# Both kv sums of a step pair ahead of both numerators, and a PSUM copy of the counts in the picks

## The chip, the cores and the metric

The kernel runs on one core of a Trainium2 chip. The metric is the device time of one execution in microseconds (us). The engines are TensorE (PE; its weight loads are shown apart as PEld), VectorE (DVE), ScalarE (ACT), GpSimd (POOL) and SyncE (SP), which issues most of the DMAs.

## What is computed

Linear attention with random features, and then a mixture of experts on its output. Cut to what matters:

```
phi(x):  proj = x @ w_phi                    # 64 -> 128 features
         proj = proj - max|proj| over features
         [exp(proj), exp(-proj)]             # 256 features
q_p, k_p = phi(q), phi(k)                    # 8 batches, 8 heads, 576 tokens
kv  = sum over tokens of k_p (outer) v       # 256 x 64 for each head
z   = sum over tokens of k_p
num = q_p @ kv                               # the numerators
den = q_p @ z + 1e-6
x   = num / den, as 4608 rows of 512
row is computed if x @ w_skip > 0; expert e = argmax(x @ w_gate) of 8
y   = gate * (relu(x @ w1[e]) @ w2[e]);  out = x + y for computed rows, else x
```

## The kernel before

**Units and steps.** The attention stage works on units: one batch, four heads, either of k or of q. There are 16 units of each kind, and each has five steps `i`: step 0 is the tail of 64 tokens a head, steps 1 to 4 are the main part (two pairs of heads, two halves of 256 tokens). Two streams of steps run at once, that of k and, six steps behind, that of q. The time step `t` counts through them.

**Stages of a step.** Each step passes through stages with fixed lags (`run_stage(lag, f)` picks the step whose turn it is): transposes of the inputs on DVE (`st_t`, L324 and L322); the projection on PE into one PSUM tile "P" for both streams (`st_proj`, L347), its largest absolute value and the subtraction of it on DVE (L354, L357); exponentials on ACT (for k L372 and L373, and sums of them for z on POOL, L380 to L386; for q PE first transposes, L393, then L399 and L400); and last the stage of use, `f_use`.

**Stage of use.** For a k step, `st_use_k` adds to the kv sum in PSUM bank "K" (L415; the tail's part L422 after steps 2 and 4), and after step 4 ACT copies the finished sum out (L426). For a q step, `st_use_q` makes the numerators and denominators in a PSUM bank "O" (L513; the tail of two batches together, in odd batches only, L492). Then `norm` on DVE adds 1e-6 (L464), inverts (L468) and multiplies (L475, L476), which frees the bank. There are two banks "O"; the z sums (L433), the stage that turns kv into the operand `kva` (L446, L450, copied by ACT at L451 and L454), the ranking of routed rows (L613, L657) and the picks use them too.

**Pairs.** From `t` = 8 to 77 two time steps are emitted together as a pair, in the order of the list `PAIR`: a letter is a stage and the number is the step of the pair. Its stage of use is `('U', 0), ('U', 1)`, and each `U` runs the k step and then the q step. So PE has: kv sum of the first step, numerators of the first, kv sum of the second, numerators of the second. Since a unit has five steps and the streams are six apart, the pairs repeat in five kinds: with numerators of the steps q 0,1 (kv sums k 1,2), q 2,3 (k 3,4), q 4,0 (k 0,1), q 1,2 (k 2,3) and q 3,4 (k 4,0). Step 0 of k has no kv sum of its own, and step 0 of q has numerators only in odd batches.

**Who sets the order.** Within `tc.manual_schedule` (from `t` = 8 to before 79) PE and ACT keep the order of the text. DVE, POOL and SP are ordered by a planner at build time, which estimates when each instruction is ready. Each engine carries out its instructions in order.

**Picks.** When the routed rows of the first six batches are counted, two experts are picked for early work (`pick(0)` at `t` = 77, within the pair of `t` = 76, and `pick(1)` at `t` = 79). A pick sums the counts `Stot` over partitions with one matmul into a bank "O" (L689). DVE then reads the counts three times (L695 for the largest, L696, and at L703 for the part that is taken) between other small steps (L697 to L700), and works out places and gathers (L706 to L720). The bank comes free after L703.

After the attention the expert stage begins at some 340 us: it loads weights by the chunk, splits them on ACT, DVE and POOL, and does the matmuls.

Of the kernel before, what the change touches and what calls it, by code (L numbers as in the profile page):

```python
# [11 lines left out]
I32 = mybir.dt.int32  # L12
# [6 lines left out]
P = 128  # L19
# [5 lines left out]
def kernel(  # L25
# [12 lines left out]
    nc = tc.nc  # L38
    B, H, S, D = q.shape
    NF = w_phi.shape[1]  # L40
    E = w_gate.shape[1]
# [23 lines left out]
    const = ctx.enter_context(tc.tile_pool(name="const", bufs=1))  # L65
# [14 lines left out]
    def bank(tag):  # L80
        if not ps:
            return psa.tile([P, 512], F32, tag=tag, name="ps_" + tag, bufs=CFG["na"][tag])
        return ps[0].tile([P, 512], F32, tag=tag, name="ps_" + tag, bufs=NB[tag])
# [17 lines left out]
    ones_b = const.tile([P, P], BF16, name="ones_b")  # L101
# [11 lines left out]
    Stot = const.tile([P, E], BF16, name="Stot")  # L113
# [3 lines left out]
    eid0 = const.tile([1, 3], I32, name="eid0")  # L117
    idg0 = const.tile([P, 3, 2], I32, name="idg0")
    pad0 = const.tile([P, 3, 2], I32, name="pad0")
    const.tile([1, 64], I32, name="spare")  # L120
    mark = const.tile([1, 32], I32, name="mark")[:, 0:1]

    ft = const.tile([P, NSL, 4], I32, name="ft")
# [132 lines left out]
    with actx:  # L256
# [17 lines left out]
        for b in range(B):  # L274
            for kind in ("k", "q"):
                for hq in range(NQ):
                    u = Unit()
# [260 lines left out]
        def sm(tag, shape, dt=F32, bufs=2):  # L538
            return small.tile([P] + shape, dt, tag=tag, name=tag, bufs=bufs)
# [145 lines left out]
        def pick(j):  # L685


            cn = bank("O")[:, 0:E]
            nc.tensor.matmul(cn, ones_b, Stot, start=True, stop=True)  # L689
            mx = sm("mx", [5])[:, 0:1]  # L690
            d = sm("d", [5, E])[:, 0]
            key = sm("key", [5, E])[:, 0]
            km = sm("km", [5])[:, 0:1]
            pk = pks[:, j]
            nc.vector.tensor_reduce(out=mx, in_=cn, axis=AX.X, op=ALU.max)  # L695
            nc.vector.tensor_tensor(out=d, in0=cn, in1=mx.broadcast_to([P, E]), op=ALU.subtract)  # L696
            nc.vector.scalar_tensor_tensor(out=key, in0=d, scalar=0.0, in1=desc, op0=ALU.is_equal, op1=ALU.mult)  # L697
            nc.vector.tensor_reduce(out=km, in_=key, axis=AX.X, op=ALU.max)
            nc.vector.tensor_tensor(out=pk, in0=key, in1=km.broadcast_to([P, E]), op=ALU.is_equal)
            nc.vector.tensor_scalar(  # L700
                out=eid0[:, j:j + 1], in0=km[0:1], scalar1=-1.0, scalar2=float(E), op0=ALU.mult, op1=ALU.add)
            cs = sm("cs", [E])
            nc.vector.scalar_tensor_tensor(out=cs, in0=cn, scalar=float(SLOT), in1=pk, op0=ALU.min, op1=ALU.mult)  # L703
            r = slice(32 * j, 32 * j + 1)
            with nc.allow_low_precision(reason="integers up to 256 are exact"):
                nc.vector.tensor_tensor(out=Stot[r], in0=Stot[r], in1=cs[r], op=ALU.subtract)  # L706
            a4 = acc4.rearrange("p (e s) -> p e s", s=4)
            a2 = acc.rearrange("p (e s) -> p e s", s=2)
            po = pk.rearrange("p (e o) -> p e o", o=1).broadcast_to([P, E, 2])
            tp = sm("tp", [2, E], bufs=1)  # L710
            ea = sm("ea", [2], bufs=1)
            nc.vector.tensor_tensor(
                out=tp.rearrange("p s e -> p e s"), in0=(a2 if j else a4)[:, :, 0:2], in1=po, op=ALU.mult)
            nc.vector.tensor_reduce(out=ea, in_=tp, axis=AX.X, op=ALU.add)
            places(idg0[:, j], pad0[:, j], ea)
            early.append(gather_rows(idg0[:, j], SLOT, NTE * P))
            if j == 0:
                nc.vector.tensor_tensor(out=a2, in0=a4[:, :, 2:4], in1=a4[:, :, 0:2], op=ALU.subtract)
                nc.vector.tensor_tensor(out=a2, in0=a2, in1=po, op=ALU.mult)
                nc.vector.tensor_tensor(out=a2, in0=a2, in1=a4[:, :, 0:2], op=ALU.add)  # L720
# [8 lines left out]
        n = len(streams[0][0])  # L729
        LP, LE, LU, LZ, LA = CFG["lag"]  # L730
        OFF = CFG["off"]
        streams = [(x[0], x[1], 0 if j == 0 else OFF) for j, x in enumerate(streams)]
        for dh in range(2):
            nc.scalar.dma_start(
                out=wsrc[dh * 64:dh * 64 + 64],
                in_=w_phi)
# [3 lines left out]
        def run_stage(lag, f):  # L740
            for items, us, off in streams:
                s = now[0] - off - lag
                if 0 <= s < n:
                    f(*items[s])

        def f_use(u, i):
            (st_use_k if u.kind == "k" else st_use_q)(u, i)

        def f_exp(u, i):
            (st_exp_k if u.kind == "k" else st_exp_q)(u, i)  # L750
# [9 lines left out]
                    if i == 0 and s // 5 + 1 < len(us):  # L760
                        st_load(us[s // 5 + 1])

        PAIR = [('L', 0), ('T', 0), ('T', 1), ('q', 0), ('k', 0), ('P', 0), ('P', 1), ('Z', 0), ('L', 1), ('q', 1), ('A', 0), ('k', 1), ('U', 0), ('U', 1), ('D', 0), ('D', 1)]
        man = None
        for t in range(n + OFF + LA):
            if CFG["man"] and t == CFG["man"][0]:
                man = ExitStack()
                man.enter_context(tc.manual_schedule(engines={mybir.EngineType.PE, mybir.EngineType.Activation}))
            if CFG["man"] and t == CFG["man"][1]:
                man.close()  # L770
            first = 8 <= t < 78 and (t - 8) % 2 == 0
            if 8 <= t < 78 and not first:
                continue
            for c, dt in PAIR if first else [(c, 0) for c in "L" + CFG["order"] + "D"]:
                now[0] = t + dt
                if c == "L":
                    for w, f in [x for x in later if x[0] <= now[0]]:
                        later.remove((w, f))
                        f()
                elif c in "ZA":  # L780
                    lag, f = (LZ, st_z) if c == "Z" else (LA, st_aug)
                    for lg in (LZ, LA) if first else (lag,):
                        run_stage(lg, f)
                elif c == "U":
                    run_stage(LU, f_use)
                elif c in "Eqk":
                    run_stage(LE, lambda u, i: f_exp(u, i) if c in ("E", u.kind) else None)
                elif c == "P":
                    st_proj()
                elif c == "D":  # L790
                    run_stage(LU - 3, lambda u, i: st_loadv(u) if (i == 0 and u.kind == "k") else None)
                    run_stage(CFG["vtl"], lambda u, i: st_loadvt(u) if (i == 0 and u.kind == "k") else None)
                else:
                    f_t()
            if t == CFG["at"]:
                setup_aug()
            if t == 1:
                setup()
# [175 lines left out]
    start = {"E": 0, "D": 0, "C": NSD, "S": NS2}  # L974
# [134 lines left out]
    for grp in CFG["seq"]:  # L1109
# [7 lines left out]
        for which, w, n in how:  # L1117
            for _ in range(n):
                x = slots[which]
                c = done.get((x, w), 0)  # L1120
# [34 lines left out]
    T, ready, parted = [], [], []  # L1155
# [46 lines left out]
    with tc.manual_schedule():  # L1202
# [4 lines left out]
        for k, (w, x, c) in enumerate(steps):  # L1207
            kind, i = x
# [95 lines left out]
```

## Time and profile before

| What | Value |
|---|---|
| Time, median of 3 runs | 605.47 us (602.71 to 608.13) |
| The profiled execution: time, span | 607.32 us, 605.4 us |
| Mean granted TensorE clock | 0.975 |
| Attention stage | from 0 to some 340 us |

A row of a group or a wait names engine, line and tiles as out<-in; a wait has its sum in us, the number of times and the longest. A row of the timeline has its start and its length in us, then engine, line, operation and tiles, and xN where N instructions of the same kind are merged; in brackets stands the engine's idle time ahead of it and what ended it. The busy time of an engine is the union of its instructions; matmuls overlap, so the start of the next group tells more of a group's cost than its length.

### The profile page before, as it was taken

To read this page: it belongs to the slowest core of one execution; us is meant where nothing else is said; L and a number is where in the kernel's file an instruction comes from. 1 tells how busy PE (TensorE), PEld (TensorE's weight loads), DVE (VectorE), ACT (ScalarE), POOL (GpSimd) and SP (SyncE) were. 2 spreads that over 40 slices of the span, in tenths; PEclk is the share of its full clock that TensorE was granted. 3 is DMA by queue.
4 is the path that set the end of the run, shared out by engine and by line. 5 is a ranking of instruction groups with operands and counts; after the bars stand their busy time and mean duration, and the time that the engine had idled before them with its cause. 6 is when DMAs were issued, how large, how long until landed. Compare 5 with 4: busy or idle time off the path is not lost. (4 is left out here: it accounts for less than half of the span.)

```text
span 605.4 us, 18715 instructions
## 1 busy us (share of the span) xinstructions
PE 561.3 (93%) x7486; PEld 469.8 (78%) x7486; DVE 498.1 (82%) x1085; ACT 329.0 (54%) x649; POOL 375.4 (62%) x399
## 2 busy tenths in 40 slices
PE   4699999999999999999789799899999998999993
PEld 2477887777877788777667799798998987988892
DVE  5779998999989999899898749866789887867841
ACT  3266665665556555565453544345658665656720
POOL 5465567586675866848665635995567674638021
PEclk9799999999999999999899899899999999999997
DMA  9898898876778657521335297489787688777500
GB/s 158 155 156 166 190 196 181 189 135 138 164 160 189 124 142 180 121 74 46 106 106 184 71 300 268 155 289 310 202 284 227 232 288 297 244 224 261 193 20 30
DMA packets 250233, 108.33 MB, mean 179 GB/s; under 512 B 192417, under 2 KB 235553, under 8 KB 250144
## 3 DMA queue, kind: packets, MB, share of 16 engines
q1 hardware_dynamic: 245632, 97.58, 61.7%
q0 software_dynamic: 3200, 9.45, 4.3%
q8 instruction: 60, 0.98, 0.7%
q10 hardware_dynamic: 1312, 0.08, 0.1%
q14 instruction: 29, 0.24, 0.1%
HBM read 83.86 MB, written 24.02 MB: 178 GB/s over the span
## 5 line engine op out<-in xcount | busy, mean ns | idle before, releaser
L380 POOL TENSOR_TENSOR z<-ek 128x512 f32<-128x512 f32 x64 | 81.1, 1274 | 83.1 <-ACT ek L373 66.0
L200 POOL TENSOR_TENSOR w<-wraw_c,w 128x256 fp32r<-128x256 f32 x108 | 98.8, 947 | 49.6 <-ACT w L195 49.5
L195 ACT ACTIVATE w<-wraw_c 128x1024 fp32r<-128x1024 f32 x96 | 97.8, 1051 | 5.8 <-DMA wraw_c<-in_moe_w_dram 5.8
L200 DVE TENSOR_TENSOR w<-wraw_c,w 128x1024 fp32r<-128x1024 f32 x69 | 91.7, 1344 | 9.4 <-ACT w L195 8.2
L354 DVE TENSOR_REDUCE m<-ps_P 128x8 f32<-128x1024 f32 (+2 forms) x86 | 88.7, 1032 | 2.8 <-PE ps_P L347 2.8
L357 DVE TENSOR_TENSOR u<-ps_P,m 128x1024 f32<-128x1024 f32 (+2 forms) x86 | 88.5, 1029 | 2.3
L347 PE MATMUL ps_P<-wsrc,xT 64*64 64x128 f32 x2048 | 75.2, 283 | 14.2 <-DVE u L357 7.3
L513 PEld LDWEIGHTS ps_O<-kva,eq 128*64 128x64 f32 x2048 | 74.6, 138 | 16.3 <-DVE cs L703 4.7
L513 PE MATMUL ps_O<-kva,eq 128*64 128x74 f32 x2048 | 77.6, 230 | 6.7 <-DVE cs L703 4.1
L399 ACT ACTIVATE eq<-ps_U 128x512 f32<-128x512 f32 x64 | 38.2, 596 | 83.5 <-PE ps_U L393 82.5
L347 PEld LDWEIGHTS ps_P<-wsrc,xT 64*64 64x64 f32 x2048 | 59.5, 138 | 25.8 <-issue 14.7
L415 PE MATMUL ps_K<-ek,v 128*64 128x256 f32 x512 | 70.3, 394 | 0.0
L889 POOL DMA_INDIRECT out_dram<-o,si x22 | 32.4, 1474 | 57.1 <-DVE si L888 50.5
L956 PE MATMUL ps_O<-w,hh 128*128 128x512 f32 x160 | 64.2, 401 | 0.5 <-DVE o L903 0.5
L637 POOL TENSOR_SCALAR OP<-iota_p,rkp,wcol 128x128 bf16<-128x128 f32 x62 | 48.6, 795 | 13.4 <-DVE rec L468 7.2
L324 DVE STREAM_TRANSPOSE xT<-raw 128x512 f32<-128x512 f32 x64 | 43.9, 697 | 8.6 <-PE ps_P L347 4.5
L393 PE MATMUL ps_U<-ident,u 128*128 128x128 f32 x288 | 49.7, 291 | 0.3 <-DVE den L464 0.3
L372 ACT ACTIVATE ek<-u 128x512 f32<-128x512 f32 x64 | 41.0, 641 | 16.5 <-DVE u L357 9.7
L960 PE MATMUL ps_O<-w,hh 128*128 128x512 f32 x120 | 47.4, 395 | 0.1
L961 PE MATMUL ps_O<-w,hlo 128*128 128x512 f32 x120 | 47.3, 394 | 0.0
L415 PEld LDWEIGHTS ps_K<-ek,v 128*64 128x64 f32 x512 | 33.5, 139 | 16.5 <-issue 7.1
L386 POOL TENSOR_TENSOR z<-z,ekt 64x512 f32<-64x512 f32 x32 | 40.8, 1275 | 5.2 <-DMA xg<-xrows,idg 2.9
(254 smaller groups left out, 1203.6 us busy)
## 6 DMA issues: line engine op xcount, KB each, us to landing
wraw_c<-in_moe_w_dram SPq DMA_DIRECT2D x96, 512.0 KB, 5.3
raw<-in_k_dram SPq DMA_DIRECT2D x64, 144.0 KB, 3.2
raw<-in_q_dram SPq DMA_DIRECT2D x64, 144.0 KB, 3.6
v<-in_v_dram SPq DMA_DIRECT2D x64, 128.0 KB, 2.8
out_dram<-xm SPq DMA_DIRECT2D x16, 512.0 KB, 5.2
xrows<-xm SPq DMA_DIRECT2D x8, 516.0 KB, 3.9
xrows<-xm SPq DMA_DIRECT2D x8, 512.0 KB, 4.6
vt<-in_v_dram SPq DMA_DIRECT2D x32, 32.0 KB, 3.5
```

Of the source, the lines that this page charges most:

```text
L195: nc.scalar.activation(out=hi, in_=raw, func=AF.Copy)
L200: eng.tensor_tensor(out=lo[:, r], in0=raw[:, r], in1=hi[:, r].bitcast(F32), op=ALU.subtract)
L347: nc.tensor.matmul(p[s * 64:s * 64 + 64, hd, (nj + j) * NF:(nj + j + 1) * NF], xT[r, g * P + s * 64:g * P + s * 64 + 64], wsrc[r], start=T ...
L354: nc.vector.tensor_reduce(out=m.rearrange("p (j h) -> p j h", h=2), in_=pv, axis=AX.X, op=ALU.max, apply_absolute_value=True)
L357: nc.vector.tensor_tensor(out=uu[:, 0:2 * nj, :].rearrange("p (j h) f -> p j h f", h=2), in0=pv, in1=m.rearrange("p (j h o) -> p j h o", h ...
L380: zeng.tensor_tensor(out=z, in0=e[:, 0:2, :], in1=e[:, 2:4, :], op=ALU.add)
L393: nc.tensor.transpose(t[:, tt * P:(tt + 1) * P], uu[:, tt, :], ident)
L415: nc.tensor.matmul(o[hd * 64:hd * 64 + 64, :], u.v[:, 2 * hd + pr, g * D:(g + 1) * D], u.e[i][:, 2 * j + hd, :], start=(g == 0), stop=False,)
L513: nc.tensor.matmul(ov[s * 64:s * 64 + 64, 2 * j + hd, :], e[:, half, j, hd, s * 64:s * 64 + 64], kva[:, half, 2 * pr + hd, :], start=(half ...
L637: (nc.vector if last else nc.gpsimd).tensor_scalar(out=OP[:, t0 + t, c, :], in0=iota_p, scalar1=rkp[:, t:t + 1], scalar2=wcol[:, NT:NT + 1 ...
L956: nc.tensor.matmul(y[sub], hh[:, t], wh[:, fi, :], start=first, stop=False)
L960: nc.tensor.matmul(y[sub], hh[:, t], wl[:, fi, :], start=False, stop=False)
```

## The change

The stage of use is split. In a pair, `u` runs the k steps alone and `n` the q steps alone, so PE has now: kv sum of the first step, kv sum of the second, numerators of the first, numerators of the second. Outside the pairs the stage `U` is as it was. In `pick` the matmul's result is copied from PSUM to a new small tile in SBUF with one DVE copy, and the three reads go to that tile. The tile takes 2 x 32 bytes a partition, and an unused spare tile is made 64 bytes smaller.

```diff
-    const.tile([1, 64], I32, name="spare")
+    const.tile([1, 48], I32, name="spare")
...
-            cn = bank("O")[:, 0:E]
-            nc.tensor.matmul(cn, ones_b, Stot, start=True, stop=True)
+            cp = bank("O")[:, 0:E]
+            nc.tensor.matmul(cp, ones_b, Stot, start=True, stop=True)
+            cn = sm("cn", [E])
+            nc.vector.tensor_copy(out=cn, in_=cp)
...
-        PAIR = [('L', 0), ('T', 0), ('T', 1), ('q', 0), ('k', 0), ('P', 0), ('P', 1), ('Z', 0), ('L', 1), ('q', 1), ('A', 0), ('k', 1), ('U', 0), ('U', 1), ('D', 0), ('D', 1)]
+        PAIR = [('L', 0), ('T', 0), ('T', 1), ('q', 0), ('k', 0), ('P', 0), ('P', 1), ('Z', 0), ('L', 1), ('q', 1), ('A', 0), ('k', 1), ('u', 0), ('u', 1), ('n', 0), ('n', 1), ('D', 0), ('D', 1)]
...
-                elif c == "U":
-                    run_stage(LU, f_use)
+                elif c in "Uun":
+                    run_stage(LU, lambda u, i: f_use(u, i) if c == "U" or (c == "u") == (u.kind == "k") else None)
```

## The prediction

> **What bounds the kernel now.** I read the page first, then the busy time by stretches, the waits of TensorE (PE) and of VectorE (DVE), and last the timeline around single pairs and around the two picks.
>
> ```profile
> span 605.4 us, 18715 instructions
> PE 561.3 (93%) x7486; PEld 469.8 (78%) x7486; DVE 498.1 (82%) x1085; ACT 329.0 (54%) x649; POOL 375.4 (62%) x399
> 75.71:153.07 77.36, 74.74 (x1489) 60.36 (x1487) 73.32 (x182) 46.07 (x109) 54.71 (x51) 1.00 0.80 171
> ```
>
> The third row has a stretch, its length, the busy time of PE, its weight loads, DVE, ACT and POOL, then granted clock, DMA share and GB/s. It is one period of the attention stage: ten pairs, two batches, in 77.36 us (7.7 us a pair). PE is busy 74.74 of them and DVE 73.32, so both are nearly full: what is given back to one counts only where the other is not the later one. ACT and POOL have room. The change lies in these pairs, which run to about 297 us; the expert stage behind 340 us is not touched.
>
> ```profile
> PE ps_O L513 <- DVE cs L703: 4.1, 2, 3.1
> PE ps_O L513 <- ACT kva L454: 2.3, 7, 0.3
> PE ps_O L492 <- ACT kva L454: 0.9, 3, 0.3
> DVE den L464 <- PE ps_O L513: 2.5, 6, 0.4
> ```
>
> These are PE's waits from 20 to 330 us and, in the last row, DVE's from 40 to 285 us (sum, times, longest). Three of PE's rows are what the change can reach: numerators (L513, L492) that wait for the kva copies, 2.3 + 0.9 = 3.2 us, and for the picks' last read of their PSUM bank, 4.1 us.
>
> **The reordering: PE's own time.** I name a pair by the steps of its numerators (0 is the tail, L492). The kv sums are L415 and L422. This is pair q 1,2 at 95.9 us:
>
> ```profile
> 95.91 1.08 PE L415 MATMUL ps_K<-ek,v 128*64 128x256 f32 x8
> 96.82 0.60 PE L422 MATMUL ps_K<-ekt,vt 128*64 128x256 f32 x4
> 97.25 1.20 PE L513 MATMUL ps_O<-kva,eq 128*64 128x74 f32 x32
> 98.28 1.03 PE L415 MATMUL ps_K<-ek,v 128*64 128x256 f32 x8
> 99.14 1.20 PE L513 MATMUL ps_O<-kva,eq 128*64 128x74 f32 x32
> 100.27 0.66 PE L393 MATMUL ps_U<-ident,u 128*128 128x128 f32 x4
> 266.19 1.95 PE L415 MATMUL ps_K<-ek,v 128*64 128x256 f32 x16
> 267.97 0.60 PE L422 MATMUL ps_K<-ekt,vt 128*64 128x256 f32 x4
> 268.40 1.20 PE L513 MATMUL ps_O<-kva,eq 128*64 128x74 f32 x32
> 104.48 2.22 PE L513 MATMUL ps_O<-kva,eq 128*64 128x74 f32 x64
> 106.63 0.66 PE L393 MATMUL ps_U<-ident,u 128*128 128x128 f32 x4
> ```
>
> From first start to the start of what follows it takes 100.27 − 95.91 = 4.36 us. The other rows show the new sequence in places where the present kernel has it already (a step without tail work on one side): 16 sums before the sums' tail take 267.97 − 266.19 = 1.78, the tail 268.40 − 267.97 = 0.43, two numerators in a row 106.63 − 104.48 = 2.15; together 4.36 us. PE's own work costs the same in either order: 0.
>
> **The reordering: what becomes late.** The first numerator starts later by the second sum: 99.14 − 98.28 = 0.86 us, and 0.43 more where that sum has its tail (pairs q 2,3 and q 0,1). DVE's norm (L464, L468, L475, L476) follows it:
>
> ```profile
> 98.21 0.92 DVE L357 TENSOR_TENSOR u<-ps_P,m 128x768 f32<-128x768 f32 x1
> 99.05 0.15 DVE L464 TENSOR_SCALAR den<-ps_O 128x4 f32<-128x4 f32 x1
> 100.39 0.16 DVE L464 TENSOR_SCALAR den<-ps_O 128x4 f32<-128x4 f32 x1 [0.42 <-PE ps_O L513]
> 158.21 1.20 PE L513 MATMUL ps_O<-kva,eq 128*64 128x74 f32 x32
> 160.04 1.23 DVE L357 TENSOR_TENSOR u<-ps_P,m 128x1024 f32<-128x1024 f32 x1
> 161.28 0.15 DVE L464 TENSOR_SCALAR den<-ps_O 128x4 f32<-128x4 f32 x1
> 150.58 1.42 PE L492 MATMUL ps_O<-kva,eqt 128*64 128x74 f32 x31 [0.30 <-ACT kva L454]
> 154.52 0.15 DVE L464 TENSOR_SCALAR den<-ps_O 128x4 f32<-128x4 f32 x1
> 166.71 1.25 PE L513 MATMUL ps_O<-kva,eq 128*64 128x74 f32 x32 [0.33 <-ACT kva L454]
> 169.44 0.15 DVE L464 TENSOR_SCALAR den<-ps_O 128x4 f32<-128x4 f32 x1
> ```
>
> In pair q 2,3 (158.21) the numerator ends at 159.41 and the norm starts at 161.28, behind DVE's subtraction of the second projection (L357): 1.87 us of slack against 0.86 + 0.43 = 1.29. In q 0,1 the slack is 154.52 − 152.0 = 2.5 against 1.29, in q 4,0 169.44 − 167.96 = 1.48 against 0.86. Only q 1,2 is short: 99.05 − 98.45 = 0.60 against 0.86. The norm there would start about 0.3 later, and DVE loses nothing, because before the second norm it stands 0.42 us anyway until the second numerator ends, and that end does not move: the idle time goes from before the second norm to before the first. That takes DVE's order as it is; PE and ACT have theirs by hand, DVE's is laid by the planner, but the norms come behind both subtractions in the program's text too. Pair q 3,4 has no second sum and stays as it is.
>
> What becomes early: the second kv sum, by 98.28 − 97.25 = 1.03 us. Its input is two ACT exponentials from earlier in the pair, its v was loaded pairs ago, and no row of PE's waits names either. ACT's copy of a finished sum (L426) moves forward with it; ACT's next work is an exponential that waits for PE's next transposes, so nothing follows. This stage issues no DMA, and SP and POOL have nothing moved past them.
>
> **The kva waits.** In the rows at 150.58 and 166.71 the numerator comes straight behind the kva copies, or with one sum between. Now one or two sums (0.86 us or more) stand there first, so all ten waits, 3.2 us, should go. But the norms behind those numerators start 1.5 to 2.5 us after them: DVE is the later engine there, and PE only runs further ahead. Bounds: −3.2 us if PE set the pace, 0 if DVE does; I take 0, by the slack in these rows.
>
> **The picks.** Each pick holds one of the two "O" banks from its matmul to L703, and the second numerator of the pair wants that bank.
>
> ```profile
> 292.96 0.16 DVE L696 TENSOR_TENSOR d<-ps_O,mx 128x8 f32<-128x8 f32 x1
> 293.97 1.10 DVE L699 TENSOR_TENSOR pks<-key,km 128x8 f32<-128x8 f32 x1
> 295.33 2.24 PE L513 MATMUL ps_O<-kva,eq 128*64 128x74 f32 x32 [3.11 <-DVE cs L703]
> 297.62 0.16 DVE L464 TENSOR_SCALAR den<-ps_O 128x4 f32<-128x4 f32 x1 [1.24 <-PE ps_O L513]
> 299.12 0.71 DVE L324 STREAM_TRANSPOSE xT<-raw 128x512 f32<-128x512 f32 x1 [0.56 <-PE ps_P L347]
> 305.69 1.25 PE L513 MATMUL ps_O<-kva,eq 128*64 128x74 f32 x32 [0.94 <-DVE cs L703]
> 302.00:306.00 4.00, 3.06 (x62) 2.07 (x63) 3.93 (x13) 3.17 (x7) 3.84 (x4) 1.00 0.00 0
> 295.33:298.70 3.37, 3.37 (x48) 3.05 (x52) 1.93 (x15) 0.15 (x1) 2.16 (x2) 0.58 0.17 32
> 93.47 0.19 DVE L661 COPY acc<-ps_O 128x32 f32<-128x32 f32 x1 [0.46 <-PE ps_O L657]
> 303.03 1.18 DVE L697 SCALAR_TENSOR_TENSOR key<-d,desc 128x8 f32<-128x8 f32 x1
> 291.23 2.48 POOL L380 TENSOR_TENSOR z<-ek 128x512 f32<-128x512 f32 x2
> 293.79 1.26 POOL L384 TENSOR_TENSOR z<-z 128x512 f32<-128x512 f32 x1
> ```
>
> (i) Bank freed early. PE stands 3.11 us at the first pick, and the granted clock is 0.58 in the 3.37 us behind it, where 32 numerators take 2.24 us instead of 1.20. With the bank free after one copy both should go. What reaches the end is DVE's idle time that this causes: 1.24 us before the norm and 0.56 before the next transpose, together **−1.80**. At the second pick PE stands 0.94 us, but DVE is busy 3.93 of the 4.00 us around it, so nothing is late for DVE there: bounds −0.94 and 0, taken 0.
>
> (ii) The copies. Two PSUM copies; the trace has none of 8 columns, the nearest is L661's of 32 columns, 0.19 us. **+0.38**, all on DVE.
>
> (iii) The later reads. d (L696) and cs (L703) read the counts from SBUF now, so both of their inputs lie there. d from PSUM took 0.16; but small steps with both inputs in SBUF took 1.10 (L699) and 1.18 (L697), and they end where one of POOL's adds ends: L699 at 295.07, the add of 293.79 at 295.05. So four instructions may each wait for an add. Bounds: 0 (as from PSUM) to 4 × (1.18 − 0.16) = 4.1. By these rows: at the first pick d would wait from 292.96 to the adds' end at 293.71, the key for the add up to 295.05, and pks, which had waited for that anyway, would end some 0.4 later than now; at the second pick the key and L699 stand at POOL's adds already, so about 0.2 more. **+0.6**, an estimate from these rows.
> The Trainium skill (GPSIMD Engine Reference, Key points) says the same against this change: GpSimd shares its SBUF interfaces with VectorE and contends with DVE instructions that have two SBUF inputs. It also has a rule for the change (VectorE: DVE Perf Modes, Rules for kernel authors): copy PSUM to SBUF first where many operations follow. By that rule the four reads would get cheaper, by less than the 0.16 each that they take, and the sum would be about 1 us lower; the rows of L697 and L699 speak against it.
>
> The first spare tile shrinks by what the new small tile takes; no instruction touches it: 0.
>
> **The sum.** The profiled execution took 607.32 us, 1.9 more than its span, and is 1.85 above the median of 605.47. 0 (PE's order) + 0 (late norms) + 0 (kva waits) − 1.80 + 0.38 + 0.6 = −0.8: 606.5 for that execution, and against the median 604.7. From about 340 us on the expert stage waits for the last numerators, so I count what is gained before as kept.
>
> **Rivals.**
> *PE sets the pace.* Then all of PE's waits count: 3.2 + 4.1, and the slow clock behind the first pick (2.24 − 1.20 = 1.0): 8.3 us, 597.2. For it: PE's 74.74 us are more than DVE's 73.32 in the period. Against it: the norms' slack above, and DVE's waits for numerators sum to 2.5 us in 245 us.
> *POOL's adds hold the picks.* All four SBUF reads wait for a whole add (4.1) and the copies come on top (0.38), while the gain falls to 0, since DVE is then still in the pick when PE's numerators are done: 605.5 + 4.5 = 610.0. It decides once d and cs cost 1.80 − 0.38 = 1.4 us more than now. For it: L697 and L699. Against it: POOL's adds leave gaps (none follows the one at 293.79), and instructions that had waited for an add do not wait twice.
> *DVE's order is laid anew, to the worse.* The planner may see other ready times and lay the first norm ahead of the second subtraction. DVE would then stand until the first numerator ends: in q 1,2 from 98.21 to 98.45 + 0.86 = 99.31, 1.1 us; in q 2,3 from 160.04 to 159.41 + 1.29 = 160.70, 0.66 us. Six of each (the waits row counts six of 0.42 in q 1,2): 10.6 us, 615.3 with the −0.8. It decides from the first pairs on, if L464 stands before L357. Against it: in every pair of this kernel it stands behind, as in the text.
> *The copy does not free the bank early:* it lands where L695 stood or behind the subtraction after it, at 292 to 293 us; the second numerator would start near 292.5 in either case, so this is nearly the forecast.
>
> **How the numbers follow.** Forecast 604.7 with 0.60; PE sets the pace, 597.2, with 0.14; POOL's adds, 610.0, with 0.13; DVE's order, 615.3, with 0.10; something unseen, such as the planner's new order after 300 us, 0.03. The forecast's own range, by its bounds −1.8 − 0.94 + 0.38 and the other way with twice the reads' estimate, and by the spread of the runs shown (602.71 to 608.13), is 602 to 608. About 1% is what a measurement of this kernel can tell from no change: under 599.4 is faster, over 611.5 slower. Faster: 0.14 and a little of the forecast's edge, 0.15. Slower: DVE's order and a little of the unseen, 0.12. Same: 0.73. The range for 8 in 10 reaches towards the first two rivals: 599 to 610.
>
> **What would show it.** In the changed profile PE's waits for kva (L454) before numerators are gone, and PE's wait for the picks is under 0.5 us at the first, with the granted clock at full behind it. In q 1,2 DVE's idle time stands before the first norm (about 0.3) and hardly before the second. In the ten-pair period nothing changes beyond 0.3 us, though PE's waits shrink: DVE stays full. d and cs show whether they read at 0.16 or wait for POOL. I am wrong if the period shortens by 0.5 us or more (PE set the pace, or DVE's order got better), if L464 comes ahead of L357, or if the numerators' stage ends later than now.

## The result and the profile after

| | Time, median (lowest to highest) | Runs |
|---|---|---|
| before | 604.88 us (602.71 to 608.13) | 18 |
| after | 608.06 us (605.89 to 612.33) | 18 |

The ratio is 1.0054, with a 95% interval from 1.0041 to 1.0068. The changed kernel is slower by some 3.2 us. That is inside the range given and under 1%, but the forecast was a gain.

The profiled execution of the changed kernel took 605.89 us and is the fastest of its 18; that of before took 607.32. So the two spans must not be compared. Stretches inside them can be, because up to the last numerators the changed kernel repeated itself within 0.06 us in a second profile (see the experiments). From the profile page of after:

```profile
PE 557.8 (92%) x7486; PEld 467.0 (77%) x7486; DVE 502.0 (83%) x1087; ACT 328.5 (54%) x649; POOL 374.3 (62%) x399
```

PE is busy 3.5 us less than before and DVE 3.9 us more. As a ruler I take the starts of the large subtractions on DVE (L357; 86 in each kernel, counted from 0). From number 22 to 72 is the pairs' stretch, from 72 to 85 the tail's stretch, with both picks in it. Busy time by stretches, first of before, then of after (columns as in the prediction):

```profile
82.68:276.47 193.79, 187.06 (x3720) 150.78 (x3714) 183.61 (x452) 115.39 (x275) 137.18 (x125) 1.00 0.68 152
276.47:332.18 55.71, 49.79 (x850) 36.93 (x848) 50.54 (x149) 26.98 (x62) 38.32 (x38) 0.97 0.34 107
```

```profile
81.24:276.96 195.72, 185.81 (x3712) 150.45 (x3712) 185.93 (x452) 115.04 (x275) 135.75 (x124) 1.00 0.70 155
276.96:333.43 56.47, 51.77 (x851) 38.26 (x848) 52.44 (x151) 26.30 (x61) 38.27 (x38) 0.94 0.34 105
```

The pairs lose 195.72 − 193.79 = 1.93 us and the tail 0.76, together 2.69 of the 3.2 measured. In the pairs DVE does the same number of instructions (452) and is busy 2.32 us longer. Fifty subtractions are two and a half of the ten-pair periods, so a period is 0.8 us longer, where the prediction allowed 0.3 for no change. What PE waits for in after, from 20 to 330 us (sum, times, longest):

```profile
PE ps_O L657 <- DVE den L464: 5.2, 3, 1.8
...
PE ps_O L433 <- POOL z L386: 1.6, 1, 1.6
PE ps_O L433 <- DVE rec L468: 1.3, 1, 1.3
```

No row of this view names kva any more, and none a pick's step. PE waits for DVE in other places instead (the first row; in before 1.9 us), and new are the waits of the z sum (L433), which has no row in this view of before. Pair q 1,2 of after, in the timeline:

```profile
97.06 2.22 PE L513 MATMUL ps_O<-kva,eq 128*64 128x74 f32 x64
98.30 0.16 DVE L464 TENSOR_SCALAR den<-ps_O 128x4 f32<-128x4 f32 x1 [0.24 <-PE ps_O L513]
99.33 0.16 DVE L464 TENSOR_SCALAR den<-ps_O 128x4 f32<-128x4 f32 x1
```

All 64 numerators stand in one row. The idle time stands before the first norm (0.24 us) and hardly before the second (99.33 − 99.05 − 0.19 = 0.09), as forecast.

**Where the pairs lose.** In the pairs q 2,3, which also rank rows (L613 to L646). The pair of an odd batch, first before (its rows at 160.04 and 161.28 stand in the prediction), then after:

```profile
155.00 0.60 ACT L399 ACTIVATE eq<-ps_U 128x512 f32<-128x512 f32 x1 [3.08 <-PE ps_U L393]
...
159.87 0.14 DVE L624 TENSOR_TENSOR Stot<-Stot,st 128x8 bf16<-128x8 bf16 x1
159.91 1.27 POOL L386 TENSOR_TENSOR z<-z,ekt 64x512 f32<-64x512 f32 x1
...
161.19 0.18 DVE L633 TENSOR_REDUCE rki<-rm 128x4 int32<-128x32 f32 x1
...
161.47 0.17 DVE L634 TENSOR_SCALAR rkp<-rki 128x4 int32<-128x4 int32 x1
161.55 0.17 DVE L640 TENSOR_SCALAR RKH<-rki 128x4 int32<-128x4 int32 x1
161.62 0.17 DVE L468 RECIPROCAL rec<-den 128x4 f32<-128x4 f32 x1
161.75 0.64 DVE L646 SCALAR_TENSOR_TENSOR rm<-RKH,OH 128x32 bf16<-128x32 int32 x4
...
163.53 1.22 DVE L354 TENSOR_REDUCE m<-ps_P 128x8 f32<-128x1024 f32 x1
```

```profile
153.14 0.60 ACT L399 ACTIVATE eq<-ps_U 128x512 f32<-128x512 f32 x1 [2.33 <-PE ps_U L393]
...
158.06 1.26 POOL L386 TENSOR_TENSOR z<-z,ekt 64x512 f32<-64x512 f32 x1
158.75 0.60 DVE L624 TENSOR_TENSOR Stot<-Stot,st 128x8 bf16<-128x8 bf16 x1
...
160.50 0.17 DVE L633 TENSOR_REDUCE rki<-rm 128x4 int32<-128x32 f32 x1
160.77 0.17 DVE L634 TENSOR_SCALAR rkp<-rki 128x4 int32<-128x4 int32 x1
160.85 0.17 DVE L640 TENSOR_SCALAR RKH<-rki 128x4 int32<-128x4 int32 x1
161.05 0.63 DVE L646 SCALAR_TENSOR_TENSOR rm<-RKH,OH 128x32 bf16<-128x32 int32 x4
161.56 0.15 DVE L464 TENSOR_SCALAR den<-ps_O 128x4 f32<-128x4 f32 x1
...
163.24 1.21 DVE L354 TENSOR_REDUCE m<-ps_P 128x8 f32<-128x1024 f32 x1
```

Two things are seen. First, the planner laid the first norm's two small steps behind the ranking's. Before, den stood between rki and rkp, and rec between RKH and rm. A small step that needs the one just ahead starts 0.18 to 0.27 us after it (160.50 to 160.77), an independent one 0.07 to 0.1 (161.47 to 161.55); den and rec had filled such gaps. From L633 to the next L354 it took 163.53 − 161.19 = 2.34 us and takes 163.24 − 160.50 = 2.74: 0.40 more. In the pairs of even batches as much is lost, but it is won back in the next pair, where DVE had stood for PE before: from the subtraction at 127.36 us to that at 134.19 it took 6.83 us, in after 6.38 (126.70 to 133.08).

Second, in the pairs of odd batches the small add into Stot (L624) takes 0.60 us instead of 0.14; two such adds lie in the pairs' stretch. This one ends at 159.35, POOL's add of 158.06 at 159.32. Before, it fell just ahead of POOL's add of 159.91. POOL is earlier because PE is. In the pair ahead, from the first kv sum to the transposes (L393) behind the numerators, PE takes 4.36 us (148.09 to 152.45); before, with a wait for kva between, it took 5.12 (149.19 to 154.31). ACT's exponentials follow at 153.14 instead of 155.00, 1.86 us earlier, while DVE's L354 ahead of L624 is only 1.11 earlier (157.64 against 158.75).

**Where the tail loses.** The timeline around the picks, before and after (lines behind L690 count two more in after):

```profile
292.08 0.96 DVE L357 TENSOR_TENSOR u<-ps_P,m 128x768 f32<-128x768 f32 x1
...
301.04 1.22 DVE L357 TENSOR_TENSOR u<-ps_P,m 128x1024 f32<-128x1024 f32 x1
...
308.69 1.23 DVE L357 TENSOR_TENSOR u<-ps_P,m 128x1024 f32<-128x1024 f32 x1
...
312.74 0.18 DVE L572 TENSOR_TENSOR d<-L,mx 128x32 f32<-128x32 f32 x1
```

```profile
291.48 2.33 PE L513 MATMUL ps_O<-kva,eq 128*64 128x74 f32 x64
292.54 0.96 DVE L357 TENSOR_TENSOR u<-ps_P,m 128x768 f32<-128x768 f32 x1
293.60 0.62 DVE L698 TENSOR_TENSOR d<-cn,mx 128x8 f32<-128x8 f32 x1
299.87 1.22 DVE L357 TENSOR_TENSOR u<-ps_P,m 128x1024 f32<-128x1024 f32 x1
301.38 0.62 PE L433 MATMUL ps_O<-z,ones_f 128*32 128x256 f32 x4 [1.29 <-DVE rec L468]
302.34 1.26 POOL L386 TENSOR_TENSOR z<-z,ekt 64x512 f32<-64x512 f32 x1 [3.28 <-ACT ek L373]
303.65 1.07 PE L433 MATMUL ps_O<-z,ones_f 128*32 128x256 f32 x4 [1.65 <-POOL z L386]
307.63 1.23 DVE L357 TENSOR_TENSOR u<-ps_P,m 128x1024 f32<-128x1024 f32 x1
310.29 0.95 POOL L213 DMA_INDIRECT xg<-xrows,idg  x1 [0.30 <-issue]
310.65 1.93 DVE L572 TENSOR_TENSOR d<-L,mx 128x32 f32<-128x32 f32 x1
311.25 1.28 POOL L380 TENSOR_TENSOR z<-ek 128x512 f32<-128x512 f32 x1
302.60:309.40 6.80, 5.75 (x68) 4.46 (x72) 6.67 (x13) 2.08 (x6) 6.41 (x6) 0.50 0.00 0
```

The last row is one of the busy time by stretches. The first pick gives what it promised: its numerators run on without a wait, and from its subtraction to the next large one it takes 299.87 − 292.54 = 7.33 us instead of 301.04 − 292.08 = 8.96, a gain of 1.63. But from the subtraction at 307.63 to the stretch's end (333.43) it takes 25.80 us, before 332.18 − 308.69 = 23.49: 2.31 go there. PE, no longer late, now stands at the z sum, twice, and the granted clock is 0.50 in the 6.80 us from 302.60 on; DVE is busy 6.67 of these, so most of it is hidden. Openly on DVE's path stands L572 with 1.93 us instead of 0.18. The planner laid it ahead of the next largest value (L354, at 312.51); before, it stood behind that one (311.61). There it meets an add on POOL and ends 0.05 us after it (311.25 + 1.28 = 312.53). Between the two subtractions around it (307.63 to 313.84, before 308.69 to 312.93) 1.97 of the 2.31 us are lost.

### The profile page after: what moved, and what is told of

The parts are those of the page before. It is cut to its first block, busy times and chain, and to the rows that moved or that the text cites. A ratio compares the mean times of both kernels' runs of the same rounds, so it can differ in the third digit from the quotient of the medians.

```text
span 603.9 us, 18716 instructions
## 1 busy us (share of the span) xinstructions
PE 557.8 (92%) x7486; PEld 467.0 (77%) x7486; DVE 502.0 (83%) x1087; ACT 328.5 (54%) x649; POOL 374.3 (62%) x399
## 5 line engine op out<-in xcount | busy, mean ns | idle before, releaser
L354 DVE TENSOR_REDUCE m<-ps_P 128x8 f32<-128x1024 f32 (+2 forms) x86 | 88.6, 1031 | 2.8 <-PE ps_P L347 2.8
L357 DVE TENSOR_TENSOR u<-ps_P,m 128x1024 f32<-128x1024 f32 (+2 forms) x86 | 88.4, 1028 | 2.2
L513 PEld LDWEIGHTS ps_O<-kva,eq 128*64 128x64 f32 x2048 | 73.3, 138 | 10.4 <-DVE rm L631 3.1
L513 PE MATMUL ps_O<-kva,eq 128*64 128x74 f32 x2048 | 75.9, 229 | 2.8 <-DVE rm L631 2.0
L415 PE MATMUL ps_K<-ek,v 128*64 128x256 f32 x512 | 69.0, 396 | 0.0
L891 POOL DMA_INDIRECT out_dram<-o,si x22 | 31.1, 1415 | 55.8 <-DVE si L890 49.2
L393 PE MATMUL ps_U<-ident,u 128*128 128x128 f32 x288 | 49.4, 290 | 0.0
L386 POOL TENSOR_TENSOR z<-z,ekt 64x512 f32<-64x512 f32 x32 | 40.7, 1272 | 5.6 <-ACT ek L373 3.3
```

The costliest lines, as they stand in the source:

```text
L354: nc.vector.tensor_reduce(out=m.rearrange("p (j h) -> p j h", h=2), in_=pv, axis=AX.X, op=ALU.max, apply_absolute_value=True)
L357: nc.vector.tensor_tensor(out=uu[:, 0:2 * nj, :].rearrange("p (j h) f -> p j h f", h=2), in0=pv, in1=m.rearrange("p (j h o) -> p j h o", h ...
L393: nc.tensor.transpose(t[:, tt * P:(tt + 1) * P], uu[:, tt, :], ident)
L415: nc.tensor.matmul(o[hd * 64:hd * 64 + 64, :], u.v[:, 2 * hd + pr, g * D:(g + 1) * D], u.e[i][:, 2 * j + hd, :], start=(g == 0), stop=False,)
L513: nc.tensor.matmul(ov[s * 64:s * 64 + 64, 2 * j + hd, :], e[:, half, j, hd, s * 64:s * 64 + 64], kva[:, half, 2 * pr + hd, :], start=(half ...
```

## The experiments

Theory A was that the pairs lose by DVE's order in the rank pairs and by the add into Stot; B that the copies lay the tail's order anew; C that the loss lies in the expert stage. Stretches are from the one profiled execution of each, times and ratios from all runs, each ratio against the kernel before on the same chip.

| Kernel | Median, us | Ratio, 95% interval | Pairs' stretch | Tail's stretch |
|---|---|---|---|---|
| before | 604.8 to 605.3 | 1 | 193.79 | 55.71 |
| after | 608.06 | 1.0054 [1.0041, 1.0068] | 195.72 | 56.47 |
| after, once more | 608.48 | 1.0061 [1.0038, 1.0083] | 195.78 | 56.43 |
| reordering alone | 606.56 | 1.0022 [1.0005, 1.0039] | 195.86 | 56.04 |
| copies alone | 604.40 | 0.9998 [0.9980, 1.0016] | 193.71 | 55.27 |
| old order in rank pairs | 606.16 | 1.0021 [1.0004, 1.0039] | 194.51 | 57.58 |
| copy in first pick alone | 604.38 | 0.9986 [0.9970, 1.0003] | 193.80 | 54.72 |
| den in its gap | 605.95 | 1.0022 [1.0002, 1.0042] | 194.53 | 56.40 |
| den and counts in gaps | 605.87 | 1.0005 [0.9982, 1.0028] | 193.24 | 56.47 |
| den and counts in gaps, copy in first pick alone | 603.80 | 0.9989 [0.9973, 1.0006] | 193.21 | 55.93 |
| after, z add ahead of gathers | 611.38 | 1.0110 [1.0091, 1.0129] | 195.81 | 56.82 |
| den and counts in gaps, copy in first pick alone, z add | 602.94 | 0.9964 [0.9952, 0.9977] | 193.16 | 54.05 |
| copy in first pick alone, z add | 602.58 | 0.9960 [0.9945, 0.9975] | 193.74 | 53.60 |

Times do not follow the two stretches to the microsecond. With the reordering alone they are 2.40 us longer than before and the median 1.4; with the old order in the rank pairs 2.59 and 1.0; with the z add moved in the changed kernel 3.13 and 6.05. What the stage behind them adds in each kernel, no run here shows.

**The reordering alone.** The picks and the spare tile are those of before:

```diff
-            cp = bank("O")[:, 0:E]
-            nc.tensor.matmul(cp, ones_b, Stot, start=True, stop=True)
-            cn = sm("cn", [E])
-            nc.vector.tensor_copy(out=cn, in_=cp)
+            cn = bank("O")[:, 0:E]
+            nc.tensor.matmul(cn, ones_b, Stot, start=True, stop=True)
```

> The pairs have both kv sums first, the picks are as before the change. Theory A (the loss sits in the pairs that also rank a batch's rows: the planner lays the first norm behind the rank's small steps there, about 0.4 us each of six, and in every second one the add to Stot meets a POOL add, about 0.45 us): 2.4 to 3.3 us slower than before, 607.3 to 608.2, and in the trace the subtractions L357 fall back by some 0.85 us per ten pairs from 73 to 286 us. Theory B (the loss comes from the copies, which make the planner lay the work after 300 us anew): within 1 us of before, 604 to 606. Theory C (the loss is in the expert stage, by the phase in which it starts): no fall-back in the pairs.

The whole loss of the pairs is here (195.86), without any copy. The median's 1.4 us are less than the 2.4 to 3.3 that A gave.

**The copies alone.** The list of stages is that of before:

```diff
-        PAIR = [..., ('k', 1), ('u', 0), ('u', 1), ('n', 0), ('n', 1), ('D', 0), ('D', 1)]
+        PAIR = [..., ('k', 1), ('U', 0), ('U', 1), ('D', 0), ('D', 1)]
```

> The copies in both picks alone, the pairs as before the change. Theory A: 0 to 1.6 us faster than before, 603.3 to 605.0. Theory B: 1.5 to 2.7 us slower, 606.4 to 607.6. In both, PE's stand of 3.1 us at the first pick and the slow clock behind it go.

The pairs are as before (193.71); of the picks' gain 0.44 us is left at the end of the tail (55.27), too little for the runs to tell. The time is within A's range, and the 1.5 us or more that B put on the copies didn't come. What B said of the order did come: the order on POOL in the tail is that of the changed kernel and not that of before, and L572 stands ahead of L354 here too. In all thirteen traces the same holds: L572 stands ahead of L354 in the seven of kernels that copy in both picks, and behind it in the six others.

**The old order in the rank pairs.** The changed kernel, but pairs q 2,3 have the stage `U` of before:

```diff
+        PAIR_U = PAIR[:12] + [('U', 0), ('U', 1), ('D', 0), ('D', 1)]
...
-            for c, dt in PAIR if first else ...
+            for c, dt in (PAIR_U if (t - 10) % 5 == 2 else PAIR) if first else ...
```

> The changed kernel, but the pairs with numerators q 2,3 (all that rank a batch) keep sum, numerators, sum, numerators; DVE's order in them is then that of before. Theory A: the 2.5 to 3.3 us come back, 604.8 to 605.6. Theory B: as the changed kernel, 608. A half of it each way would say that only the waits for kva or the other pairs matter.

The pairs' stretch falls to 194.51: 1.21 of the 1.93 us come back. This changes PE's order and DVE's there together, so it does not say which. The add into Stot still takes 0.60 us in the odd batches (at 159.38 and 237.25), although its pair has the old order: PE runs ahead in the pairs between, and POOL with it. So the rest of the loss stays. The tail, whose text is the changed kernel's, came out 1.1 us longer, and the median is neither A's nor B's.

**The copy in the first pick alone**, and the rest as before:

```diff
+            cn = cp
+            if j == 0:
+                cn = sm("cn", [E])
+                nc.vector.tensor_copy(out=cn, in_=cp)
```

> The copy in the first pick alone, the second as before the change, the pairs as before. All that is laid behind the second pick stays as it was. Theory A and B: PE's 3.1 us and DVE's idle 1.8 us at the first pick go, less 0.6 for the copy and the reads: 1.0 to 1.8 us faster than before, 603.1 to 603.9. If POOL's adds hold the pick's reads: no gain or up to 1 us slower.

The tail's stretch is 54.72, 0.55 less than with both copies. That is 0.99 us less than before, and the median 0.8, a little less than forecast; the interval of the ratio just reaches 1.

**The changed kernel once more**, beside the next three.

> The changed kernel once more, beside the variants below. All theories: slower than before by 0.3 to 0.7%. In the profile the stretch from the 22nd to the 72nd of the large subtractions on DVE (some 50 to 292 us after the start of the span, to be called the pairs' stretch) is 195.7 us long again, against 193.8 before; if it is 194.0 or less, the loss in the pairs was chance and the order of DVE has nothing to do with it.

Both stretches come out within 0.06 us of the first time. So the loss in the pairs is no chance.

**DVE's order mended, PE's kept.** The rest of `rank` is traced behind den, with an edge on DVE that holds it there; the count goes with it. PE, ACT, POOL and SP keep the changed kernel's order to the instruction:

```diff
-            nc.vector.tensor_scalar(
-                out=den.rearrange("p (t o) -> p t o", o=1), in0=o[:, :, NA1:NAUG],
-                scalar1=1e-6, scalar2=None, op0=ALU.add,
-            )
+            den_i = nc.vector.tensor_scalar(out=den.rearrange("p (t o) -> p t o", o=1), in0=o[:, :, NA1:NAUG], scalar1=1e-6, scalar2=None, op0=ALU.add)
+            while pend:
+                with tc.issue_after(den_i.ins):
+                    list(pend.pop(0))
...
-                nc.vector.tensor_scalar(out=rkp[:, 0:nt], ...
+                yield; nc.vector.tensor_scalar(out=rkp[:, 0:nt], ...
...
-                for n, f in zip(CFG["post"], (rank, index, rest)):
+                for n, f in zip(CFG["post"], (lambda: (pend.append(rank()), next(pend[-1])), index, rest)):
```

> The changed kernel, with the two steps den (L464) ahead of rkp (L634) in the pairs that rank rows, and the count's two steps (L623, L624) among the steps behind it. PE, ACT, POOL and SP keep the changed kernel's order to the instruction. Theory A (DVE's order in the rank pairs: latency gaps left open, and the add into Stot that meets POOL's adds): the pairs' stretch falls back from 195.7 to 193.5 to 194.0 us, and the time by some 1.9 us against the changed kernel, ratio to before about 1.002. Rival P (the order on PE: first numerators come later): the stretch stays at 195.4 or more. Rival K (PE's vanished waits for kva are worth something once DVE's order is mended): the stretch falls below 193.0.

Its pairs' stretch, and three steps of the rank pair:

```profile
81.08:274.32 193.24, 185.26 (x3712) 150.26 (x3711) 183.70 (x452) 115.16 (x275) 136.30 (x125) 1.00 0.69 154
```

```profile
159.44 0.15 DVE L464 TENSOR_SCALAR den<-ps_O 128x4 f32<-128x4 f32 x1
159.62 0.17 DVE L634 TENSOR_SCALAR rkp<-rki 128x4 int32<-128x4 int32 x1
...
160.16 0.15 DVE L624 TENSOR_TENSOR Stot<-Stot,st 128x8 bf16<-128x8 bf16 x1
```

The add into Stot is back at 0.15 us, DVE's busy time at 183.70, and the stretch at 193.24: 2.48 us less than after with the same order on PE. So A holds, though the stretch fell by 0.26 us more than its range, and P, that PE's new order costs time, falls. The stretch is also 0.55 under that of before, and K's bound of 193.0 is not reached. These 0.55 us are not all due to the vanished waits for kva, since the count's steps have left their old places too. Counted from one subtraction to the next, 0.28 of them lie behind the two pairs of even batches, where DVE stands for PE (0.48 us at 130.80, before 0.55 at 132.50) and one small step more is laid into a gap; the other 0.27 lie where the count's steps were moved. The waits for kva are worth 0.28 us at the most.

**den alone in its gap.** The same, with the count ahead of the `yield`, so that it stays where the changed kernel has it.

> As the last one, but the count's two steps stay where the changed kernel has them; nothing but den (L464) and rec (L468) moves, in six pairs. Theory A: the latency gaps close (0.40 us in each of six pairs), but in the three pairs of even batches the gain is lost again, since PE's index sum waits for POOL there anyway; so the stretch shrinks by about 1.2 us, to 194.5, and the add into Stot still takes 0.6 instead of 0.14 us in the three odd ones. Rival: if the add's collision is the whole cause, the stretch stays at 195.4 or more; if the gaps are the whole cause, it falls to 193.8.

194.53, as A said: the gaps are 1.2 us of the loss, and the add into Stot, which still takes 0.6 us, is most of the rest (194.53 − 193.24 = 1.29): between the subtractions around the two adds lie 0.9 of these 1.29 us. The other 0.4 come with the count's new place.

**The mended order with one copy.** The second pick reads PSUM again:

```diff
-            cn = sm("cn", [E])
-            nc.vector.tensor_copy(out=cn, in_=cp)
+            cn = sm("cn", [E]) if j == 0 else cp
+            j or nc.vector.tensor_copy(out=cn, in_=cp)
```

> The mended order with the copy in the first pick alone. Theory A and B together (the pairs lose by DVE's order, the tail by what the second copy does to the planner's order): pairs' stretch 193.5 to 194.0, and behind it about 1 us less than before, as with the copy in the first pick alone: ratio to before 0.998, and faster than both kernels. Rival (the tail's order depends on anything ahead of it, not on the second copy): behind 292 us it loses 0.5 to 3 us as the other variants did, ratio 1.000 to 1.004.

The pairs are as with both copies (193.21, a little under the range given). The tail is 55.93: not the 54.72 that the same single copy gave behind the old pairs. So it does depend on what stands ahead of it, as the rival says, but it is only 0.22 us longer than before, and the ratio lies between the two forecasts. The order isn't the reason that the rival took: on POOL it is the same as with the single copy alone, and L572 stands behind L354 in both. What differs is which small steps POOL's adds hold: here pks and tp of the second pick (1.21 and 1.24 us, there 0.17 and 0.18), there L572 (2.17 us, here 0.18).

**POOL's z add ahead of the gathers.** Theory Z: the z sum's wait is for an add (L386) that POOL does behind the first pick's two gather issues (L213). An edge on POOL puts the gathers behind the add; no other engine's order moves:

```diff
-            early.append(gather_rows(idg0[:, j], SLOT, NTE * P))
+            late_gather(j) if j == 0 else early.append(gather_rows(idg0[:, j], SLOT, NTE * P))
...
-                zeng.tensor_tensor(out=z[r], in0=z[r], in1=u.e[0][r], op=ALU.add)
+                zlast[0] = zeng.tensor_tensor(out=z[r], in0=z[r], in1=u.e[0][r], op=ALU.add)
...
+        def gather0(): exec_after(zlast[0], lambda: early.append(gather_rows(idg0[:, 0], SLOT, NTE * P)))
```

> The changed kernel, but on POOL the last add of the z sum (L386) stands ahead of the first pick's two gather issues (L213) instead of behind them. Nothing else moves on any engine. The tail's stretch is that from the 72nd to the 85th large subtraction on DVE (some 277 to 333 us): 56.4 us in the changed kernel, 55.7 before. Theory Z (what the first pick gives PE is lost at the z sum L433, which waits for that add, and in the slow clock behind this wait): the 1.65 us wait at L433 goes, the 32 numerators behind it take 1.2 instead of 2.24 us, and the tail's stretch falls to 54.0 to 55.0; the time falls by 1.5 to 2.5 us against the changed kernel, ratio to before 1.001 to 1.003. Rival C (the add then meets the pick's own steps, which read two tiles of SBUF): those behind L701 wait up to 1.27 us, and the stretch stays at 56 or more. Rival D (DVE sets the pace there and PE's wait is hidden): the wait goes, the stretch stays within 0.3 of 56.4.

In the changed kernel it makes things worse: the ratio is 1.0110, where Z had 1.001 to 1.003. Three of its rows:

```profile
296.29 1.27 DVE L714 TENSOR_TENSOR tp<-acc,pks 128x16 f32<-128x16 f32 x1
303.07 0.64 PE L433 MATMUL ps_O<-z,ones_f 128*32 128x256 f32 x8 [0.82 <-DVE rec L468]
310.61 1.31 PE L446 MATMUL ps_O<-aug,kvs 128*128 128x146 f32 x4 [2.59 <-DVE lgm L476]
```

The wait for POOL is gone, as Z said, but the add now holds a step of the first pick (L714, 1.27 us, as C said), and PE stands 2.59 us for DVE seven microseconds on. The stretch is 56.82, where C put it, 0.4 us longer than in the changed kernel; the time is some 3 us longer. The profiled execution (608.40 us) is the fastest of its four, the median is 3 us above it, and what the other runs lost isn't seen in it. That stays open.

**The same edge in the two kernels with one copy**, the mended one and the one with the pairs of before.

> The mended order with the copy in the first pick alone (pairs' stretch 193.2, tail's stretch 55.9), and POOL's z add ahead of the first gathers as well. Theory Z: PE's waits at the z sum there, 0.77 us and part of 1.23, go, and the tail's stretch falls to 54.5 to 55.3; pairs' stretch 193.2 as without it; ratio to before 0.995 to 0.998. Rival C or D: the tail's stretch stays at 55.7 or more, ratio 0.998 to 1.000.

> The kernel before with the copy in the first pick alone (pairs' stretch 193.8, tail's stretch 54.7), and POOL's z add ahead of the first gathers as well. Theory Z: PE's wait at the z sum, 1.22 us, goes and the tail's stretch falls to 53.5 to 54.4; ratio to before 0.995 to 0.998. Rival C: up to 1.27 us on DVE in the pick, the stretch at 54.7 to 56.0, ratio 0.998 to 1.001.

```profile
274.55:328.60 54.05, 49.43 (x858) 36.42 (x854) 50.77 (x151) 26.21 (x61) 38.59 (x39) 1.00 0.34 110
```

```profile
276.21:329.81 53.60, 48.90 (x850) 35.70 (x848) 50.20 (x149) 26.94 (x62) 38.48 (x38) 1.00 0.34 111
```

These are the tails of the two, the mended one first. Here Z's numbers come: the tail is 1.88 and 1.12 us shorter than without the edge (the first by more than Z said), at the full clock. But the mechanism in the traces is not Z's. PE waits no more for POOL at the z sum, yet it stands as long for DVE elsewhere (1.6 us for den in the first, 1.4 for the second pick's largest count in the other). What the tail gains are small steps on DVE that no longer meet an add. In the mended kernel these are pks and the add into Stot of the second pick (first two rows without the edge, then with it), in the other L572 (likewise):

```profile
299.97 1.21 DVE L701 TENSOR_TENSOR pks<-key,km 128x8 f32<-128x8 f32 x1
302.57 1.17 DVE L708 TENSOR_TENSOR Stot<-Stot,cs 1x8 bf16<-1x8 bf16 x1
301.00 0.17 DVE L701 TENSOR_TENSOR pks<-key,km 128x8 f32<-128x8 f32 x1
302.52 0.16 DVE L708 TENSOR_TENSOR Stot<-Stot,cs 1x8 bf16<-1x8 bf16 x1
308.35 2.17 DVE L572 TENSOR_TENSOR d<-L,mx 128x32 f32<-128x32 f32 x1
310.37 0.18 DVE L572 TENSOR_TENSOR d<-L,mx 128x32 f32<-128x32 f32 x1
```

The time between the two subtractions around them falls from 8.79 to 6.51 us in the first and from 6.13 to 4.22 in the second. Around the first pick both lose 1.1 us, since the add now holds tp there (1.27 us), as C said. So Z's numbers came by luck: the same edge lost in one kernel and gained in two by the steps that the adds happen to meet. Both are faster than before, 0.9964 [0.9952, 0.9977] and 0.9960 [0.9945, 0.9975], and than the changed kernel; they can't be told from each other. They do not need the change's reordering: the second has the pairs of before.

## Why the prediction was wrong

*PE's own order, 0:* right. In pair q 1,2 the six groups still take 4.36 us (94.85 to 99.21 in after).

*Late norms, 0:* the slack was read rightly, and in q 1,2 the idle time moved as said. **The step that failed stands in the sentence behind it: "That takes DVE's order as it is".** I had argued that the norms come behind both subtractions in the text, and left it at that. They still do; the planner moved the norm against the ranking, which shares the pair q 2,3 with it, and I had not taken the ranking into account. So the term that was put at 0 was +1.93 us. The two kernels that differ from the changed one in DVE's order alone show its parts, 1.2 us for the gaps and 1.3 for the rest, most of it the add into Stot. Their sum is more than the 1.93 lost, since the mended order comes out 0.55 us under that of before.

*The kva waits, bounds −3.2 and 0, taken 0:* they all went, and DVE was the later engine. With the order mended they bring 0.28 us at the most, near the end that I took. What I did not see is that PE's running ahead is no neutral thing: ACT and POOL follow PE, and POOL's adds then stood against another step of DVE.

*The picks:* the clock behind the first is full and the wait is gone. The copy takes 0.15 us at each pick, not 0.19. The SBUF reads were put at +0.6 and cost nothing at the first pick: d waits for the add as forecast (0.62 us), but from d to cs it takes 2.01 us (293.60 to 295.61), before 2.15 (292.96 to 295.11), since the steps behind d no longer wait as long. So the first pick gave 1.63 us by the next subtraction, where the sum had 0.8 for both. At the second, the add into Stot (L708) met an add of POOL and took 1.17 us, before 0.16, and by the next subtraction 0.11 us was lost.

*"I count what is gained before as kept":* the second step that failed. In the changed kernel the gain is gone within the tail, and in the kernel with the copies alone 0.44 us of it is left. PE, early now, waits at the z sum for POOL; DVE's small steps meet POOL's adds at other moments. L572 takes 1.93 or 1.94 us in both runs of after and in the two kernels with its tail and mended pairs (tails of 56.40 to 56.47), and 0.18 or 0.19 before, with the copies alone and in both kernels that are faster than before. But with the copy in the first pick alone it took 2.17, and the tail was still 54.72: there the time between the subtractions around L572 is 1.90 us longer than before, and around the two picks it is 2.00 and 0.97 shorter. In the changed kernel it is 1.97 longer around L572, 1.63 shorter and 0.11 longer around the picks, and 0.3 longer elsewhere: together the 0.76 us of the tail. That L572 stands where it does comes with the second copy. Whether it then meets an add depends on when POOL's adds run; with the copies alone it met none, and the tail lost most of the gain behind it instead. No run moves L572 alone.

*Rivals:* the nearest was "DVE's order laid anew, to the worse", given 0.10. Its mechanism came, its place did not: L464 stays behind L357 and the price is 2.5 us in the pairs, not 10.6. PE did not set the pace, and POOL's adds held the first pick no longer than before. That the loss lies in the expert stage (theory C of the experiments) has little for it: 2.69 of the 3.2 us are lost before it begins. The other 0.5 us stay open. Of the signs of being wrong, the last one came: the numerators' stage ends later.

## What to carry to other kernels

Where a planner orders an engine, a reordering on another engine can change that order too: list the small steps that share the stretch, and ask which of them fill each other's latency. On the engine that sets the pace, an independent small step between two dependent ones was worth about 0.1 to 0.2 us each time here. A wait that is taken from an engine off the critical path lets all that follows it run earlier, and so changes which adds and which small steps meet; a gain at one place counts only after the next place where the early engine must wait has been read. And a variant whose time comes out as forecast may still owe it to something else: the rows tell which steps got shorter.

## What the runs showed of the hardware

A small DVE step (8 to 32 columns, 0.14 to 0.18 us alone) takes as long as the POOL add that it meets still runs: 0.60 us (L624), 1.17 (L708 in after, at 305.03), and with the copy in the first pick alone 2.17 (L572, through two adds of 307.98 to 310.46). They end 0.02 to 0.06 us after the add. Of the 1.93 us of L572 in after, the first 0.60 lie ahead of the add, while POOL issues a gather (L213); with the copies alone the same step took 0.19 us within such an issue (307.62 in one of 307.51 to 308.48), so what held it there isn't shown. For steps with two tiles of SBUF this was forecast from the profile and the Trainium skill (GPSIMD Engine Reference, Key points). It held steps with one input tile too: with the copies alone, L223 (pad from ea, 2 columns) took 1.27 us and ended at 304.69, POOL's adds at 304.66. The same place of the Trainium skill names a 2-port mode of DVE as well, which I had left out; whether L223 runs in it, no run here shows. Reductions weren't held: L700 took 0.16 us at 294.45, within POOL's add of 294.26 (1.29 us).

PE's clock fell to 0.50 in after with no idle time longer than 1.65 us before it: 1.29 us, four matmuls, and in the second gap the clock went. The Trainium skill (TensorE: Matmul & The Clock Gate, Why this matters for your kernels) asks for no gaps above about 3 us; here shorter ones, close together, were enough.

The half clock shows little while DVE is full: the time from one subtraction to the next in after (299.87 to 307.63, 7.76 us), at half clock from 302.60 on, is only 0.11 longer than before at the full clock (301.04 to 308.69, 7.65). The second pick's steps lie otherwise in the two, so this isn't the price of the clock alone.
